# Attention by pairs of units on one core: coarser softmax stages, and a finished tile turned together with its gate logits

## The chip, the core and the metric

The kernel runs on one core of a Trainium2 chip, as one launch. Its time is device time in microseconds (us). TensorE (PE in the profile) multiplies, and its weight loads have a row of their own (PEld). VectorE is DVE, ScalarE is ACT, GpSimd is POOL, and SyncE (SP) issues most DMAs. PE, DVE, ACT and POOL each work through their own instructions in the order in which the kernel writes them.

## The reference, cut to what matters

```
scores = q @ k.T / 8;  bias = -slope[h] * |i - j|;  mask = 0 <= i - j < 128      # B 4, H 8, S 576, D 64
attn   = exp(scores + bias - max);  attn = attn / (sum(attn) + 1e-9);  x = attn @ v   # x: 2304 tokens x 512
logits = x @ w_gate + modality_bias[modality_id];  e = argmax(logits)            # 8 experts
out[e == i] = gate * (relu(x[e == i] @ w1[i]) @ w2[i])
h = out @ w_in;  result = relu(h)**2 @ w_out
```

All of it is float32. The change lies in the first two lines and in `x @ w_gate`.

## The kernel before, in words

The tokens form 18 groups of 128 rows. Each of the four batches has tiles t = 0 to 3 of 128 queries and a tail t = 4 of 64 queries; the tails of two batches share a group. A query sees at most 128 keys back, so a tile t = 1 to 3 needs 256 columns of keys, t = 0 needs 128, and the tail 192 (both heads of a pair lie on the 128 partitions of the tail, 64 queries each).

A **unit** is one tile and one head pair `hp` (two heads of 64 dimensions, which fill 128 partitions), so there are 80 units. The loop over `k` from line 792 is a pipeline written out by hand (the schedule is manual: the order in the code is the order on each engine). In step `k`:

- `sc` of unit k+1 (L220, L223): scores on PE into PSUM. For t < 4 each head is a product over 64 partitions, one on partitions 0 to 63 and one on 64 to 127.
- `smax` of unit k (L234, L236): on DVE scale, bias and row maximum in one instruction for each head, from PSUM into `x`.
- `ev` of unit k-4 (L286 to L289): ACT copies the turned weights of attention from the PSUM bank `x` to `pt`.
- `sexp` of unit k-1 (L249, L252): ACT's exp with its row sum, for each head.
- `tr` of unit k-3 (L275, L277, L278): PE turns the exponentials by 128x128 transposes into the one bank `x`.
- `norm` (L259 to L266): for the tail the division before the product, on DVE; for t < 4 only the 1e-9, on POOL.
- `background()`: one step of each open generator (the `post` of finished tiles, the routing `route`, the prefetch of the first expert).
- `pv` of unit k-5 (L306, L313): PE multiplies by V into one of two banks `v`, 64 columns of weights for each head.

When all four head pairs of a tile are in its bank `v`, `post` takes over: ACT copies the bank to a row buffer `xu` (L330); four transposes (L337) and four products with 16 gate columns (L338, into bank `m`) turn it back to tokens by 512 and give the logits by head; DVE divides both by the row sums (L349, L351), adds the heads up (L352), and SP writes the tokens to DRAM (L354).

All float32 products but the transposes run as two instructions on PE, so a product has two matmul records and two weight loads in the trace. After the loop come five expert slots and a dense layer, whose products all have line 643 in the trace. The first expert's products start inside the last steps of the loop (`FIRST_UP`, `PIECES`); loads of most expert weights start at the loop's end, when the attention's SBUF is given back (L824).

Of the kernel before, what the change touches and what calls it, by code (L numbers as in the profile page):

```python
# [8 lines left out]
F32 = mybir.dt.float32  # L9
# [3 lines left out]
AF = mybir.ActivationFunctionType  # L13
# [35 lines left out]
def attention_moe_kernel(ctx, tc, qh, kh, v, mid, wg, mb, w1, w2, win, wout, out):  # L49
# [9 lines left out]
    def ct(shape, name, dt=F32, p=const):  # L59
        return p.tile(shape, dt, name=name)  # L60
# [40 lines left out]
    wgs = ct([128, 4, 2 * E], "wgs")  # L101
# [16 lines left out]
    wk = ap("wk", 3)  # L118
# [4 lines left out]
    biast = ct([128, 4, 192], "biast", p=cst)  # L123
    mids = ct([128, 2 * NT], "mids", I32, p=cst)
# [87 lines left out]
    def sc(u):  # L212
        b, t, hp = u
        if t < 4:

            st[u] = [bank("s"), bank("t")]
            c0 = 128 if t == 0 else 0
            for j in range(2):
                r = slice(64 * j, 64 * j + 64)
                pe.matmul(st[u][j][:, c0:256], qS[b, t][r, hp, :], kS[b][r, hp, 128 * t - 128 + c0:128 * t + 128], start=True, stop=True)  # L220
        else:
            st[u] = [bank("s")]
            pe.matmul(st[u][0][:, :192], qS[b, t][:, hp, :], kS[b][:, hp, 384:576], start=True, stop=True)  # L223

    def smax(u):
        b, t, hp = u
        s = st[u]
        x = wk.tile([128, 2, 256], F32, tag="x", name="x")
        m = sm.tile([128, 2], F32, tag="m", name="m")
        kw = dict(scale=-0.125, scalar=3e38, op0=ALU.add, op1=ALU.min)  # L230
        if t < 4:
            c0 = 128 if t == 0 else 0
            for j in range(2):
                dve.tensor_tensor_reduce(out=x[:, j, c0:], in0=s[j][:, c0:256], in1=bias[:, 2 * hp + j, c0:], accum_out=m[:, j:j + 1], **kw)  # L234
        else:
            dve.tensor_tensor_reduce(out=x[:, 0, :192], in0=s[0][:, :192], in1=biast[:, hp, :], accum_out=m[:, 0:1], **kw)  # L236
        st[u] = x, m

    def sexp(u):
        b, t, hp = u  # L240
        x, m = st[u]
        st[u] = e = wk.tile([128, 2, 256], F32, tag="e", name="e", bufs=5)
        if t < 4:
            if hp == 0:
                rinv[b, t] = sm.tile([128, H], F32, tag="ri", name="ri")
            c0 = 128 if t == 0 else 0
            for j in range(2):
                h = 2 * hp + j
                act.activation(e[:, j, c0:], x[:, j, c0:], AF.Exp, bias=m[:, j:j + 1], scale=-1.0, accum_out=rinv[b, t][:, h:h + 1])  # L249
        else:  # L250
            rinv[u] = r = sm.tile([128, 1], F32, tag="rt", name="rt")
            act.activation(e[:, 0, :192], x[:, 0, :192], AF.Exp, bias=m[:, 0:1], scale=-1.0, accum_out=r)  # L252

    def norm(u, stage):
        b, t, hp = u
        if t < 4:
            if stage == 0 and hp == 3:
                r = rinv[b, t]
                pool.tensor_scalar(r, r, 1e-9, None, op0=ALU.add)  # L259
        elif stage == 0:  # L260
            dve.tensor_scalar(rinv[u], rinv[u], 1e-9, None, op0=ALU.add)
        elif stage == 1:
            dve.reciprocal(rinv[u], rinv[u])
        else:
            e = st[u]
            dve.tensor_scalar(e[:, 0, :192], e[:, 0, :192], rinv.pop(u), None, op0=ALU.mult)  # L266

    def tr(u):
        b, t, hp = u
        e = st[u]  # L270
        st[u] = p = bank("x", (128, 4, 128))
        if t < 4:
            for j in range(2):
                for i in range(1 if t == 0 else 0, 2):
                    pe.transpose(p[:, 2 * i + j, :], e[:, j, 128 * i:128 * i + 128], ident)  # L275
        else:
            pe.transpose(p[:, 0, :], e[:, 0, 0:128], ident)  # L277
            pe.transpose(p[:64, 1, :], e[:, 0, 128:192], ident)  # L278

    def ev(u):  # L280
        b, t, hp = u
        p = st[u]
        st[u] = o = wk.tile([128, 4, 128], F32, tag="pt", name="pt")
        if t < 4:
            c0 = 2 if t == 0 else 0
            act.copy(o[:, c0:, :], p[:, c0:, :])  # L286
        else:
            act.copy(o[:, 0, :], p[:, 0, :])
            act.copy(o[:64, 1, :], p[:64, 1, :])  # L289
# [4 lines left out]

    def pv(u):
        b, t, hp = u
        o = st.pop(u)
        if hp == 0:
            pvb[b, t] = bank("v", (128, 4, 128))
        w = pvb[b, t]  # L300
        kb = [4] if t == 4 else [t - 1, t] if t else [t]
        if t < 4:
            for n, k_ in enumerate(kb):
                for j in range(2):
                    h = 2 * hp + j
                    pe.matmul(w[64 * j:64 * j + 64, hp, :], vS[b][:, k_, 64 * h:64 * h + 64], o[:, 2 * (k_ - t + 1) + j, :], start=n == 0, stop=n == len(kb) - 1, skip_group_check=True)  # L306
        else:
            c = slice(64 * (b % 2), 64 * (b % 2) + 64)
            for n in range(2):
                r = 64 if n else 128  # L310
                for j in range(2):
                    h = 2 * hp + j
                    pe.matmul(w[64 * j:64 * j + 64, hp, c], vS[b][:r, 3 + n, 64 * h:64 * h + 64], o[:r, n, 64 * j:64 * j + 64], start=n == 0, stop=n == 1, skip_group_check=True)  # L313

        if u[2] == 3:
            if t < 4 or b % 2 == 0:
                xus[group(u)] = row().rearrange("p (a b) -> p a b", a=4)
            if t == 4:
                act.copy(xus[group(u)][:, :, c], w[:, :, c])

    xbusy = []
    xus = {}

    def post(u):
        b, t, _ = u
        g = group(u)
        w = pvb.pop((b, t))
        xu = xus.pop(g)
        if t < 4:
            act.copy(xu, w)  # L330
        yield
        while xbusy:
            yield
        xbusy.append(True)
# [8 lines left out]
        le = "p h e -> p e h"  # L343
        if t == 4:
            dve.tensor_copy(xs, xp.rearrange("p a b -> p (a b)"))
            dve.tensor_reduce(l_all[:, g, :], lp.rearrange(le), axis=AX.X, op=ALU.add)
        else:
            r = rinv.pop((b, t))[:, :, None]
            dve.tensor_tensor(xs.rearrange("p (h d) -> p h d", h=H), xp.rearrange("p a (c d) -> p (a c) d", d=64), r.to_broadcast([128, H, 64]), op=ALU.mult)  # L349
            ls = sm.tile([128, H, E], F32, tag="ls", name="ls", bufs=2)  # L350
            dve.tensor_tensor(ls, lp, r.to_broadcast([128, H, E]), op=ALU.mult)  # L351
            dve.tensor_reduce(l_all[:, g, :], ls.rearrange(le), axis=AX.X, op=ALU.add)  # L352
        xbusy.pop()
# [182 lines left out]
    units = [(b, t, hp) for b in range(B) for t in range(5) for hp in range(4)]  # L536
# [216 lines left out]
    FIRST_UP = 81  # L753
    PIECES = 1
# [37 lines left out]
    for k in range(n + 5):  # L792
        if k + 1 < n:
            sc(units[k + 1])
        if 0 <= k - 2 < n:
            norm(units[k - 2], 0)
        if k < n:
            smax(units[k])
        if 0 <= k - 4 < n:
            ev(units[k - 4])  # L800
        if 0 <= k - 1 < n:
            sexp(units[k - 1])
        if 0 <= k - 3 < n:
            tr(units[k - 3])
        if 0 <= k - 2 < n:
            norm(units[k - 2], 1)
        background()
        if 0 <= k - 2 < n:
            norm(units[k - 2], 2)
        if k % 4 == 1 and k // 4 + 3 < len(tiles):  # L810
            load(*tiles[k // 4 + 3])
        for at, make in ((6, tail_consts), (9, tail_bias), (11, route_consts), (15, logit_bias), (30, dump_rows)):
            if k == at:
                make()
        if 0 <= k - 5 < n:
            u = units[k - 5]
            pv(u)
            if u[2] == 3 and (u[1] < 4 or u[0] % 2):
                todo.append(post(u))
# [335 lines left out]
```

## Time and profile before

| | us |
|---|---|
| median of 3 runs (832.58 to 834.7) | 832.81 |
| the profiled execution | 831.27 |
| its span, first to last instruction | 829.6 |
| PE busy | 801.1 (97%) |
| DVE busy | 397.8 (48%) |
| ACT busy | 342.5 (41%) |
| POOL busy | 274.3 (33%) |

The profiled execution lies 1.54 us below the median. A matmul's record contains the way through the array, so records of neighbours overlap; the distance between two starts tells what one costs. "Busy" counts such an overlap once, and a PE that is busy all the time may still stand between two groups of products.

### The profile page before, as it was taken

How to read it: one execution, taken by the hardware profiler on the slowest of the kernel's cores; microseconds unless marked ns; L12 is line 12 of the kernel's file. 1: busy time of each engine (PE TensorE's matmuls, PEld its weight loads, DVE VectorE, ACT ScalarE, POOL GpSimd, SP SyncE). 2: the span in 40 equal slices, each digit the busy share in tenths (PEclk: the TensorE clock that was granted, in tenths of full speed). 3: DMA queues.
4: the chain of work that ended last, by engine and by line, in shares of the span. 5: the costliest groups of instructions: out<-in, count | busy, mean ns of one | idle time of the engine just before them, and what ended most of it. 6: DMA issues, size and time to landing. Idle time of an engine off the chain costs nothing.

```text
span 829.6 us, 13776 instructions
## 1 busy us (share of the span) xinstructions
PE 801.1 (97%) x5051; PEld 670.5 (81%) x5051; DVE 397.8 (48%) x1060; ACT 342.5 (41%) x910; POOL 274.3 (33%) x330
## 2 busy tenths in 40 slices
PE   6999999999899999989789999999999999999998
PEld 3767676777688788878678989899898989899896
DVE  3676767678988765777345432122221203131220
ACT  5877778534444444444352423223140413222230
POOL 1111033036665556554232432213050413223140
PEclk9999999999999999999899999999999999999999
DMA  6354353138565545462201021010100101010000
GB/s 217 105 176 168 124 177 135 65 115 307 190 237 172 197 167 198 168 207 73 66 22 56 26 77 52 1 52 2 39 14 0 53 0 52 1 51 1 26 1 26
DMA packets 38807, 79.11 MB, mean 95 GB/s; under 512 B 6224, under 2 KB 14672, under 8 KB 38736
## 3 DMA queue, kind: packets, MB, share of 16 engines
q1 hardware_dynamic: 35696, 68.23, 24.7%
q0 software_dynamic: 3040, 9.96, 3.2%
q8 instruction: 41, 0.67, 0.3%
q14 instruction: 30, 0.25, 0.1%
HBM read 62.19 MB, written 15.99 MB: 94 GB/s over the span
## 4 chain that ended last, share of the span: by engine, by line
PE 51%; DVE 0%; ACT 0%; issue 0%; DVEq 0%
PE t L643 19%; PE v L643 15%; PE s L643 13%; PE x L643 2%; PE m L643 1%; PE x L631 1%; PE m L631 0%; DVE w L638 0%; ACT w L636 0%; ACT w L553 0%; ACT row L1015 0%; DVE row L1031 0%; DVE w L989 0%; DVE row L993 0%; DVEq L948 0%
## 5 line engine op out<-in xcount | busy, mean ns | idle before, releaser
L643 PE MATMUL s<-w 128*128 128x256 f32 (+2 forms) x1344 | 220.8, 321 | 7.6 <-DVE h L668 6.9
L643 PEld LDWEIGHTS s<-w 128*128 128x128 f32 x1344 | 194.5, 191 | 27.3 <-DVE h L668 10.0
L643 PE MATMUL t<-w,h 128*128 128x512 f32 x888 | 214.4, 397 | 0.0
L1006 POOL TENSOR_TENSOR h<-row,h 128x256 fp32r<-128x256 f32 x144 | 109.5, 764 | 276.0 <-ACT h L1005 271.3
L643 PEld LDWEIGHTS t<-w,h 128*128 128x128 f32 x888 | 164.4, 188 | 37.8
L643 PE MATMUL v<-w,h 128*128 128x512 f32 x432 | 104.7, 396 | 0.0
L643 PEld LDWEIGHTS v<-w,h 128*128 128x128 f32 x432 | 80.2, 188 | 18.7
L554 POOL TENSOR_TENSOR w<-w 128x1024 fp32r<-128x1024 f32 x23 | 56.8, 2474 | 33.0 <-PE s L643 18.5
L1016 DVE SCALAR_TENSOR_TENSOR row<-s,row 128x256 f32<-128x256 f32 x72 | 30.5, 424 | 70.1 <-ACT row L1015 70.1
L249 ACT ACTIVATE e<-x,m 128x256 f32<-128x256 f32 (+1 forms) x128 | 60.8, 482 | 0.8 <-DVE m L234 0.8
L1005 ACT CAST h<-row 128x256 fp32r<-128x256 f32 x144 | 57.6, 400 | 4.8 <-DVE row L1016 4.8
L638 DVE TENSOR_TENSOR w<-x,w 128x512 fp32r<-128x512 f32 (+1 forms) x13 | 7.7, 606 | 90.6 <-ACT w L636 90.6
L220 PE MATMUL s<-kS,qS 64*128 64x256 f32 (+1 forms) x128 | 44.7, 436 | 6.4 <-DMA qS<-qh 6.1
L553 ACT CAST w<-w 128x1024 fp32r<-128x1024 f32 x46 | 48.0, 1049 | 6.2 <-DVE row L409 2.8
L1015 ACT ACTIVATE row<-s 128x256 f32<-128x256 f32 x72 | 27.5, 383 | 54.7 <-PE s L643 53.6
L643 PE MATMUL t<-w 128*128 128x256 f32 x384 | 48.3, 282 | 0.0
L667 ACT ACTIVATE h<-s 128x512 fp32r<-128x512 f32 (+1 forms) x40 | 23.1, 577 | 61.1 <-PE s L643 58.1
L643 PEld LDWEIGHTS t<-w 128*128 128x128 f32 x384 | 47.1, 190 | 0.3
L636 ACT CAST w<-x 128x512 fp32r<-128x512 f32 (+1 forms) x13 | 6.6, 521 | 96.3 <-PE x L631 96.3
L554 DVE TENSOR_TENSOR w<-w 128x1024 fp32r<-128x1024 f32 x26 | 42.7, 1647 | 6.9 <-ACT w L553 6.3
L286 ACT COPY pt<-x 128x512 f32<-128x512 f32 (+1 forms) x64 | 34.2, 534 | 28.4 <-PE x L275 21.1
L220 PE MATMUL t<-kS,qS 64*128 64x256 f32 (+1 forms) x128 | 44.8, 437 | 0.0
(234 smaller groups left out, 1080.4 us busy)
## 6 DMA issues: line engine op xcount, KB each, us to landing
w<-w SPq DMA_DIRECT2D x40, 512.0 KB
w<-win SPq DMA_DIRECT2D x16, 512.0 KB
w<-wout SPq DMA_DIRECT2D x16, 512.0 KB
xd<-row SPq DMA_DIRECT2D x22, 256.0 KB
qS<-qh SPq DMA_DIRECT2D x19, 256.0 KB
row<-yd SPq DMA_DIRECT2D x18, 256.0 KB
vS<-vh SPq DMA_DIRECT2D x16, 256.0 KB
out_dram<-row SPq DMA_DIRECT2D x16, 256.0 KB
```

What stands on the lines that cost most here:

```text
L220: pe.matmul(st[u][j][:, c0:256], qS[b, t][r, hp, :], kS[b][r, hp, 128 * t - 128 + c0:128 * t + 128], start=True, stop=True)
L249: act.activation(e[:, j, c0:], x[:, j, c0:], AF.Exp, bias=m[:, j:j + 1], scale=-1.0, accum_out=rinv[b, t][:, h:h + 1])
L286: act.copy(o[:, c0:, :], p[:, c0:, :])
L553: (dve.tensor_copy if quick else act.copy)(h, r)
L554: (eng or dve).tensor_tensor(l, r, h.bitcast(F32), op=ALU.subtract)
L631: pe.transpose(p[:, c, :], r[:, 128 * c:128 * c + 128], ident)
L643: pe.matmul(ps, l, r, start=first and i == 0, stop=last and i == n - 1)
L667: act.activation(hh, p, AF.Relu)
L1005: act.copy(g[:, 0:256], gt)
L1006: pool.tensor_tensor(g[:, 256:512], gt, g[:, 0:256].bitcast(F32), op=ALU.subtract)
L1015: act.activation(r, p, AF.Relu)
L1016: dve.scalar_tensor_tensor(gt, p, 0.0, r, op0=ALU.max, op1=ALU.mult)
```

## The change

The unit becomes a pair of head pairs, (b, t, hh): 40 units instead of 80. Scores of two head pairs lie in one bank (`s` and `t` are now full banks), transposes go to two banks `v`, one for each head pair, and the product with V goes to one bank `W0` that is kept for good. The pipeline has three stages fewer: `smax` and `sexp` belong to the same step, `tr` and `ev` come two steps later, `pv` three. `post` copies the tile with DVE instead of ACT, and turns it and makes its logits in one product for each head pair: the moving operand is the identity and 16 gate columns side by side, 144 columns. Three of these land in bank `m`, the fourth in the upper half of `W0`; DVE then needs two divisions from each of the two banks.

```
-    for k in range(n + 5):
-        sc(k+1); norm(k-2, 0); smax(k); ev(k-4); sexp(k-1); tr(k-3); norm(k-2, 1); background(); norm(k-2, 2); pv(k-5)
+    for k in range(n + 3):
+        smax(units[k])
+        sexp(units[k], 0)
+        norm(units[k - 1])
+        sc(units[k + 1])
+        tr(units[k - 2])
+        ev(units[k - 2], 0)
+        sexp(units[k], 1)
+        ev(units[k - 2], 1)
+        background()
+        pv(units[k - 3])
+        background()
```

The block above leaves out the bounds on k and the loads; the lines below are the diff's.

```
-    wk = ap("wk", 3)
+    wk = ap("wk", 2)
+    turned = ct([128, 4, 128 + 2 * E], "turned", p=cst)
...
-        nc.sync.dma_start(out=wgs, in_=wg)
+        nc.sync.dma_start(out=turned[:, :, 128:], in_=wg)
+        for i in range(4):
+            pool.tensor_copy(turned[:, i, :128], ident)
...
+    W0 = bank("x", (128, 4, 128))
...
-        if t < 4:
-            act.copy(xu, w)
+        dve.tensor_copy(xu[:, :, c], W0[:, :, c])
+        if t == 4 and b % 2 == 0:
+            return
...
-        xp, lp = w, bank("m", (128, H, E))
+        C = 128 + 2 * E
+        xp = bank("m")[:, :3 * C].rearrange("p (a c) -> p a c", a=3), W0[:, 2:4, :].rearrange("p a b -> p (a b)")[:, None, :C]
         for i in range(4):
-            pe.transpose(xp[:, i, :], xu[:, i, :], ident)
-            pe.matmul(lp[:, 2 * i:2 * i + 2, :], xu[:, i, :], wgs[:, i, :], start=True, stop=True)
+            pe.matmul(xp[i // 3][:, i % 3, :], xu[:, i, :], turned[:, i, :], start=True, stop=True)
...
+        for p, h0, n in ((xp[0], 0, 6), (xp[1], 6, 2)):
+            hs = slice(h0, h0 + n)
+            for o, w, d in ((xs.rearrange("p (h d) -> p h d", h=H)[:, hs, :], p[:, :, :128], D), (ls[:, hs, :], p[:, :, 128:], E)):
...
+                    dve.tensor_tensor(o, w, r[:, hs].rearrange("p (a j) -> p a j", j=2)[:, :, :, None].to_broadcast([128, n // 2, 2, d]), op=ALU.mult)
...
-    FIRST_UP = 81
-    PIECES = 1
+    FIRST_UP = 40
+    PIECES = 2
```

The next two pieces are PE's order where the scores of the second batch's tail begin: first the last steps of t = 3 with the turn of tile t = 1 before the change (`s`, `t` scores, `e` exponentials, `pt` turned, `m` logits; numbers tell buffers apart).

```order
L220 MATMUL s_1083<-kS_359,qS_730 128x256
L220 MATMUL t_1084<-kS_359,qS_730 128x256
L275 MATMUL x_1096<-ident_71,e_1040 128x128 x4
L337 MATMUL v_956<-ident_71,row_1052 128x128
L338 MATMUL m_1101<-wgs_89,row_1052 128x16
...
L306 MATMUL v_1078<-pt_1062,vS_360 64x128 x4
L223 MATMUL s_1115<-kS_359,qS_851 128x192
L275 MATMUL x_1126<-ident_71,e_1064 128x128 x4
L306 MATMUL v_1078<-pt_1091,vS_360 64x128 x4
```

The same place after the change, one step with the turn of tile t = 1 (`x_123` is `W0`).

```order
L226 MATMUL s_971<-kS_335,qS_765 128x192 x2
L289 MATMUL v_974<-ident_71,e_861 128x128 x4
L289 MATMUL v_979<-ident_71,e_861 128x128 x4
L353 MATMUL m_989<-turned_117,row_956 128x144 x3
L353 MATMUL x_123<-turned_117,row_956 128x144
L324 MATMUL x_123<-pt_943,vS_336 64x128 x8
```

Scores, turns and products with V now stand in groups of two head pairs, so PE goes from one kind to the next half as often; the eight instructions of the turn have become four.

ACT at the same place before: the copy of the tile, evictions, and exps of the unit whose maxima were found a step earlier.

```order
L330 COPY row_1052<-v_956 128x512
L286 COPY pt_1091<-x_1068 128x512
L249 ACTIVATE e_1093,ri_1065<-x_1058,m_1059 128x256 x2
L286 COPY pt_1121<-x_1096 128x512
L249 ACTIVATE e_1123,ri_1065<-x_1087,m_1088 128x256 x2
```

ACT after the change:

```order
L260 ACTIVATE e_922,ri_923<-x_916,m_917 128x256 x2
L300 COPY pt_943<-v_933 128x512
L260 ACTIVATE e_922,ri_923<-x_916,m_917 128x256 x2
L300 COPY pt_943<-v_938 128x512
L260 ACTIVATE e_968,ri_923<-x_962,m_963 128x256 x2
```

The exps now stand ahead of the step's evictions and need maxima of the same step; the copy of the tile is gone from this queue. It stands on DVE, ahead of the next step's maxima, and the turn's results are taken by four divisions instead of two:

```order
L344 COPY row_956<-x_123 128x512
L239 ISA x_962,m_963<-s_927,bias_115 128x256
...
L355 RECIPROCAL ri_728<-ri_728 128x8
L367 TENSOR_TENSOR row_1003<-m_989,ri_728 128x384
L367 TENSOR_TENSOR ls_1004<-m_989,ri_728 128x48
L367 TENSOR_TENSOR row_1003<-x_123,ri_728 128x128
L367 TENSOR_TENSOR ls_1004<-x_123,ri_728 128x16
L368 TENSOR_REDUCE l_all_72<-ls_1004 128x8
```

Before, DVE had at this place only the divisions and the sum:

```order
L340 RECIPROCAL ri_841<-ri_841 128x8
L234 ISA x_1117,m_1118<-s_1083,bias_116 128x256
...
L349 TENSOR_TENSOR row_1131<-v_956,ri_841 128x512
L351 TENSOR_TENSOR ls_1133<-m_1101,ri_841 128x64
L352 TENSOR_REDUCE l_all_72<-ls_1133 128x8
```

## Rows read from the trace of the kernel before

**Rows 1.** Windows: us busy by engine, instructions, granted clock, DMA share, GB/s.
```profile
core 0: us, PE busy (x) PEld busy (x) DVE busy (x) ACT busy (x) POOL busy (x), PEclk, DMA share, GB/s
22.00:160.00 138.00, 136.36 (x1257) 98.66 (x1253) 95.90 (x491) 106.67 (x372) 23.05 (x54) 1.00 0.42 139
160.00:240.00 80.00, 76.16 (x369) 60.07 (x368) 66.31 (x149) 32.81 (x54) 41.38 (x31) 1.00 0.58 206
```

**Rows 2.** Timeline, PE: start, duration, line, tiles, shape. One step, scores of t = 3.
```profile
66.81 0.48 PE L220 MATMUL s<-kS,qS 64*128 64x256 f32 x1
67.13 0.38 PE L220 MATMUL s<-kS,qS 64*128 64x256 f32 x1
67.45 0.66 PE L275 MATMUL x<-ident,e 128*128 128x128 f32 x4
68.03 0.66 PE L306 MATMUL v<-pt,vS 128*64 128x128 f32 x8
68.62 0.48 PE L220 MATMUL s<-kS,qS 64*128 64x256 f32 x1
```

**Rows 3.** Timeline, PE: scores of 128 columns, t = 0.
```profile
78.81 0.37 PE L220 MATMUL s<-kS,qS 64*128 64x128 f32 x1
79.02 0.27 PE L220 MATMUL s<-kS,qS 64*128 64x128 f32 x1
79.23 0.33 PE L277 MATMUL x<-ident,e 128*128 128x128 f32 x1
```

**Rows 4.** Timeline, PE: first units of the kernel, four units' scores in one run.
```profile
3.77 0.55 PE L220 MATMUL s<-kS,qS 64*128 64x128 f32 x1 [3.77 <-DMA qS<-qh]
4.11 0.42 PE L220 MATMUL s<-kS,qS 64*128 64x128 f32 x1
4.33 0.42 PE L220 MATMUL s<-kS,qS 64*128 64x128 f32 x1
4.54 0.42 PE L220 MATMUL s<-kS,qS 64*128 64x128 f32 x1
```

**Rows 5.** Timeline, PE: units of a tail, t = 4.
```profile
71.53 0.59 PE L223 MATMUL s<-kS,qS 128*128 128x192 f32 x2
71.95 0.60 PE L275 MATMUL x<-ident,e 128*128 128x128 f32 x4
72.48 0.66 PE L306 MATMUL v<-pt,vS 128*64 128x128 f32 x8
```

**Rows 6.** Timeline, PE: the turn of a finished tile.
```profile
69.25 0.66 PE L275 MATMUL x<-ident,e 128*128 128x128 f32 x4
69.75 0.27 PE L337 MATMUL v<-ident,row 128*128 128x128 f32 x1
69.86 0.29 PE L338 MATMUL m<-wgs,row 128*128 128x16 f32 x2
70.00 0.31 PE L337 MATMUL v<-ident,row 128*128 128x128 f32 x1
70.94 0.66 PE L306 MATMUL v<-pt,vS 128*64 128x128 f32 x8
```

**Rows 7.** Timeline, ACT: an eviction and a unit's two exps.
```profile
70.00 0.58 ACT L286 COPY pt<-x 128x512 f32<-128x512 f32 x1
70.48 0.51 ACT L249 ACTIVATE e<-x,m 128x256 f32<-128x256 f32 x1
70.99 0.50 ACT L249 ACTIVATE e<-x,m 128x256 f32<-128x256 f32 x1
```

**Rows 8.** Timeline, DVE: a unit's two maxima, with the wait ahead of them.
```profile
67.66 0.42 DVE L234 CUSTOM_DVE_ANT_0 x<-s,bias 128x256 f32<-128x256 f32 x1 [1.03 <-PE t L220]
68.01 0.42 DVE L234 CUSTOM_DVE_ANT_0 x<-t,bias 128x256 f32<-128x256 f32 x1
```

**Rows 9.** Groups by line and form, DVE, 18 to 160 us: busy, mean ns, idle before.
```profile
L349 DVE TENSOR_TENSOR row<-v,ri 128x512 f32<-128x512 f32 x15 | 10.4, 692 | 11.0 <-PE v L337 4.3 <-ACT pt L286 4.2 <-PE t L220 1.7
L352 DVE TENSOR_REDUCE l_all<-ls 128x8 f32<-128x64 f32 x15 | 4.0, 267 | 0.5
L351 DVE TENSOR_TENSOR ls<-m,ri 128x64 f32<-128x64 f32 x15 | 3.2, 215 | 0.0
L345 DVE COPY row<-v 128x512 f32<-128x512 f32 x1 | 0.7, 691 | 0.5 <-PE v L337 0.5
```

**Rows 10.** Waits, 22 to 160 us: total us, times, longest.
```profile
DVE x L234 <- PE t L220: 15.5, 27, 1.0
PEld x L275 <- ACT pt L286: 8.9, 21, 1.0
```

More of the change, by code (lines that the diff above doesn't have):

```diff
@@ L254, in norm @@
[L254 to L257, printed above, removed]
+                h = 4 * hh + 2 * i + j
+                act.activation(e[:, i, j, c0:], x[:, i, j, c0:], AF.Exp, bias=m[:, i, j:j + 1], scale=-1.0, accum_out=rinv[b, t][:, h:h + 1])
+        else:
+            act.activation(e[:, i, 0, :192], x[:, i, 0, :192], AF.Exp, bias=m[:, i, 0:1], scale=-1.0, accum_out=rinv[u][:, i:i + 1])
+        if i:
+            st[u] = ex.pop(u)
+    def norm(u):
+        b, t, hh = u
+        if t < 4:
+            if hh:
@@ L268, in tr @@
+        dve.reciprocal(r, r)
+        for i in range(2):
+            dve.tensor_scalar(e[:, i, 0, :192], e[:, i, 0, :192], r[:, i:i + 1], None, op0=ALU.mult)
     def tr(u):
-        b, t, hp = u
+        b, t, hh = u
         e = st[u]
[L271 to L283, printed above, removed]
+        st[u] = ps = []
+        for i in range(2):
+            p = bank("v", (128, 4, 128))
+            ps.append(p)
+            if t < 4:
+                for j in range(2):
+                    for k_ in range(1 if t == 0 else 0, 2):
+                        pe.transpose(p[:, 2 * k_ + j, :], e[:, i, j, 128 * k_:128 * k_ + 128], ident)
+            else:
+                pe.transpose(p[:, 0, :], e[:, i, 0, 0:128], ident)
+                pe.transpose(p[:64, 1, :], e[:, i, 0, 128:192], ident)
@@ L284, in ev @@
+        ex[u] = wk.tile([128, 2, 4, 128], F32, tag="pt", name="pt")
+    def ev(u, i):
+        b, t, hh = u
+        p, o = st[u][i], ex[u]
         if t < 4:
             c0 = 2 if t == 0 else 0
[L286 removed]
+            act.copy(o[:, i, c0:, :], p[:, c0:, :])
         else:
[L288 to L289 removed]
+            act.copy(o[:, i, 0, :], p[:, 0, :])
+            act.copy(o[:64, i, 1, :], p[:64, 1, :])
+        if i:
+            st[u] = ex.pop(u)
@@ L534, in attention_moe_kernel @@
     second = []
-    units = [(b, t, hp) for b in range(B) for t in range(5) for hp in range(4)]
+    units = [(b, t, hh) for b in range(B) for t in range(5) for hh in range(2)]
     tiles = [(b, t) for b in range(B) for t in range(5)]
@@ L791, in attention_moe_kernel @@
     hidden = []
-    for k in range(n + 5):
+    for k in range(n + 3):
+        now, last = k < n, 0 <= k - 2 < n
+        if now:
+            smax(units[k])
+            sexp(units[k], 0)
+        if 0 <= k - 1 < n:
+            norm(units[k - 1])
         if k + 1 < n:
             sc(units[k + 1])
[L795 to L806, printed above, removed]
-        background()
[L808 to L812, printed above, removed]
+        if last:
+            tr(units[k - 2])
+            ev(units[k - 2], 0)
+        if now:
+            sexp(units[k], 1)
+        if last:
+            ev(units[k - 2], 1)
+        background()
+        if k >= 3:
+            pv(units[k - 3])
+        background()
+        if k % 2 == 0 and k // 2 + 3 < len(tiles):
+            load(*tiles[k // 2 + 3])
+        for at, make in ((3, tail_consts), (4, tail_bias), (5, route_consts), (7, logit_bias), (15, dump_rows)):
             if k == at:
                 make()
[L815 to L819, printed above, removed]
         if k >= FIRST_UP and primed:
```

141 lines of the change are left out of this document (66 added, 75 removed).

## The prediction

> **What bounds the kernel now.** I read the windows first. From 22 to 160 us, the attention, PE is busy for 136.4 of 138 us, DVE for 95.9 and ACT for 106.7 [rows 1]. So PE decides here, and what it is busy with has to be read from the distances between starts. The timeline of one step shows them: scores start at 66.81, turns at 67.45, products with V at 68.03, the next scores at 68.62 [rows 2]: 0.64 + 0.58 + 0.59 = 1.81 us for each unit. None of the three is filled. The turn's eight instructions follow each other in 0.11 us (69.75, 69.86) [rows 6], and the four transposes of the tail's step span 0.60 us with a last one of about 0.27 [rows 5, 6], again 0.11 apart, so four need 0.44 us and get 0.58. The eight of V span 0.66 us [rows 2], with the same last one 0.056 apart; they need 0.45 and get 0.59. Scores of 256 columns take 0.32 for each of the two instructions of a head (66.81, 67.13, 67.45) [rows 2] and of 128 columns 0.21 (78.81, 79.02, 79.23) [rows 3]: 0.11 us for 128 columns and 0.10 on top of every instruction. What is too long always comes where PE goes over to products of another shape: 64 rows for the scores, 128x128 for the turns, 128x64 for V. In the tail, where scores and turns have one shape, two scores of 192 columns take 0.42 [rows 5], which is 2 x 0.16 by columns and 0.10 left for one change. Of the waits, PE's own one for data is small: 8.9 us for the bank `x` in 21 places [rows 10], a part of which is the same change of shape.
>
> **The change, part by part.**
>
> *Fewer changes of shape.* A unit of t < 4 has three, together 0.14 (before V) + 0.14 (after V) + 0.21 (around the scores) = 0.49 us; a tail unit has two. Counted in the order of instructions up to the first expert, it is 223 changes before and 119 after; among the latter are 11 new ones, where routing or the first expert's turns now follow V. So 104 go, at 0.49 / 3 = 0.163 us: 17.0 us. The disputed part is the 0.21 around the scores. If the 0.10 on top belongs to each instruction, a pair of head pairs pays it as before, and only 0.28 of 0.49 is saved: 104 x 0.093 = 9.7 us. The startup speaks against that: four units' scores stand there in one run, the first instruction takes 0.34 (3.77 to 4.11), the next ones 0.22 and 0.21 [rows 4], so only the first carries the extra. These rows are of the slow start of the kernel, where 0.21 us is twice what 128 columns cost later, so the proof is not complete; I take 17.0 and keep 9.7. The Trainium skill, "TensorEngine Tiling (Array Packing)", Key Properties, says that changing the tiling mode drains TensorE, and a change of tile within a mode does not; by that rule all of the extra is the change's and this term is the 17.0, by the other reading of the warm rows 9.7.
>
> *The start.* Up to 22 us the PE rows are slower and the first loads are waited for (3.77 us) [rows 4]. I count nothing for the first four pairs: 4 x 0.5 = 2 us back.
>
> *The turn with the logits.* Before, from 69.75 to 70.94, 1.19 us with the change to V in it; without the 0.14 it is 1.05, about 0.09 for each of twelve instructions. After, four products of 144 columns, each of two instructions. By the slope of rows 2 and 3 one takes 144 x 0.105 / 128 = 0.12, eight 0.95: 0.1 us won for each of 18 groups, 1.8 us. Upper bound: 0.105 each as for a transpose of 128 columns, 0.84, 3.8 us won. Lower bound: 0.21 as the tail's scores with their change counted in [rows 5], 1.68, 11.3 us lost. I take 1.8, since rows 6 show loads of 128x128 weights every 0.09 us and so no reason for 0.21.
>
> *What goes to DVE.* The copy of the tile (0.69 us as in the one copy of this size [rows 9]) moves from ACT to DVE: 16 full and 4 half ones, 12.5 us. The two divisions become four; the columns are the same, so what is added is two fixed shares: 0.15 us each, from 0.215 for 64 columns against 0.692 for 512 [rows 9], so 18 x 0.3 = 5.4 us. DVE goes from 95.9 to 113.8 us in a stretch which, after the terms above, has about 120 us. It was 69% busy (95.9 of 138) and is then 95%. That is near enough to full that its order matters. By steps of a tile of t = 1 to 3, from the end of its V products: copy 0.25 to 0.9; maxima of the next pair (four, 0.35 us apart [rows 8]) to 2.3; then the divisions, which wait for the turn's products on PE (scores 1.05, transposes 1.0, turn 0.95, so 3.2) and take 1.35 us to 4.6; next maxima to 6.0; and PE reaches the end of the tile's second step at about 7.1. ACT needs 0.48 for an eviction and 0.51 for an exp [rows 7], four exps and two evictions for a pair, 3.0 us; its exps start at 5.4, when the first maxima are there, and its last eviction ends at 8.4, and PE wants it at 8.7, behind the next scores and transposes. So it just fits, with 0.3 us in hand, and routing (some 20 small DVE instructions for three tiles) falls mostly into DVE's two idle pieces (2.3 to 3.2 and 6.0 to 7.3). What does not fall there PE waits for. From both sides: nothing, or 20 tiles x 0.55 = 11 us, if all the idle time that DVE has in front of the divisions (11.0 us in 15 places [rows 9]) has to be kept. I take 4, by the 0.3 us in hand.
>
> *The rest.* The four POOL copies for the moving operand and the loads on SP stand in the first steps, where POOL is nearly idle (23 of 138 us later [rows 1]): nothing, at most 1 us. The bank `x` that PE waited for is now two banks `v`: 0 to 4 us won, and I take 0, since the turn of the first expert now needs the same two banks. What follows the attention keeps its order and starts with it; PE is the busiest there too (76.2 of 80 us, DVE 66.3 [rows 1]), and the loads of the expert weights start when the loop ends, so I let it shift as a whole.
>
> Sum: -17.0 + 2 - 1.8 + 4 = -12.8 us. The profiled execution of 831.27 becomes 818.5; it stands 1.54 below the median of 832.81, so on the median's scale **820 us**.
>
> **The rivals.**
>
> *DVE and ACT become the bound.* For it: 95% of DVE, exps that now need maxima of the same step, evictions behind the exps, one bank `W0` that must be copied before the next V products. Against it: DVE waits for PE's scores now (15.5 us in 27 places [rows 10]) and that time can be filled. Worked out: DVE's 113.8 us, and 20 us that stay idle because every tile waits once 1 us for its turn's products, make 134 of the 138 us: a gain of 4 to 7 us, 826 to 829. The Trainium skill, "TensorEngine Tiling (Array Packing)", PSUM Bottleneck, warns of this: after a faster TensorE the copies out of PSUM may bound, and both ACT and DVE should take them; here DVE takes the tile's copy alone, and no run here shows yet what that does.
>
> *The extra belongs to instructions, not to changes.* Then 9.7 instead of 17.0: 827. For it: 0.32 twice in a row in rows 2. Against it: rows 4 and the tail.
>
> *Slower: PE waits in each tile for the copy of `W0`.* One bank holds the result of V; PE can't go on with the next tile's V until DVE has read it, and the copy stands in DVE's queue behind routing and the divisions, which wait for PE themselves. In my steps the copy ends at 0.9 us and V wants the bank at 3.2 + 0.2, so 2.5 us are in hand. It decides from the point where DVE runs 2.5 us late. At 3.5 us late (one tile's copy, divisions and maxima, 0.65 + 1.35 + 1.4, not caught up) PE stands 1.0 us in each of 20 tiles, 20 us: 820 + 20 = 840.
>
> *No change.* The turn at its lower bound (11.3 lost instead of 1.8 won) takes the gain nearly away: 820 + 13.1 = 833.
>
> **How the numbers follow.** The forecast 0.55 (813 to 825), DVE and ACT 0.18, the extra by instruction 0.10, the turn 0.06, the wait for `W0` 0.11. About 0.3% of the time, 2.5 us, is what can be told from no change. The first three are faster by more than that, the 829 of the second just so: 0.82 for faster, 0.07 for the same (the turn, and a little of the second), 0.11 for slower. The range runs from 809 (no wait of PE instead of 4 us, no loss at the start instead of 2, the turn at 3.8 won: 820 - 8 = 812, and 3 of the up to 4 us of the second bank) to 830, which takes in the second and third case; the wait for `W0` and part of the turn stay outside.
>
> **What would show it.** In the profile after: scores of two head pairs at 0.21 us an instruction inside a group and 0.10 to 0.2 more at its ends; eight transposes in 1.0 us, sixteen V instructions in 1.0; eight instructions of the turn in 0.95. Steps of a pair of about 3.1 us, 4.1 with a turn. The stretch that ends at 160 us here ends near 147. PE waits for ACT's evictions below 5 us in all. Wrong it would be if PE shows waits for `pt` or for `row` copied from `W0` in every tile, if DVE stands between 95 and 100% while PE's groups have holes, or if the gain at the end of the attention shrinks before 400 us.

## The result, and the profile after

The changed kernel takes 825.16 us (median; 823.71 to 828.75) against 832.69 us for the kernel before on the same chip: a ratio of 0.9916, 95% interval 0.9892 to 0.9940. Run twice more beside the experiments it gave 0.9932 (0.9908 to 0.9957) and 0.9908 (0.9883 to 0.9934). So it is faster by 0.8%, about 7.5 us, inside the range and short of the 820 us by 5. The 12.8 us of the forecast came to little more than half, and the question is where the rest went.

The windows of the changed kernel answer to [rows 1]; columns as there.

```profile
core 0: us, PE busy (x) PEld busy (x) DVE busy (x) ACT busy (x) POOL busy (x), PEclk, DMA share, GB/s
22.00:160.00 138.00, 130.29 (x1231) 103.76 (x1230) 108.84 (x546) 95.45 (x348) 20.23 (x42) 0.99 0.42 142
160.00:240.00 80.00, 72.80 (x317) 57.49 (x316) 67.92 (x131) 31.63 (x51) 46.43 (x33) 0.98 0.60 211
```

PE is no longer full: 7.7 us idle of 138, and 7 of 80 behind. The groups themselves came as worked out. PE's timeline of the changed kernel, a turn, a tail step and scores of 256 columns, answers to [rows 2, 5, 6] (of the scores the instructions of one bank):

```profile
61.70 0.90 PE L353 MATMUL m<-turned,row 128*128 128x144 f32 x6
62.44 0.41 PE L353 MATMUL x<-turned,row 128*128 128x144 f32 x2
62.77 1.09 PE L324 MATMUL x<-pt,vS 128*64 128x128 f32 x16
...
64.55 1.04 PE L289 MATMUL v<-ident,e 128*128 128x128 f32 x8
65.52 1.09 PE L324 MATMUL x<-pt,vS 128*64 128x128 f32 x16
66.54 0.37 PE L224 MATMUL s<-kS,qS 64*128 64x128 f32 x1
...
72.80 0.48 PE L224 MATMUL s<-kS,qS 64*128 64x256 f32 x1
73.12 0.38 PE L224 MATMUL s<-kS,qS 64*128 64x256 f32 x1
73.33 0.38 PE L224 MATMUL s<-kS,qS 64*128 64x256 f32 x1
73.55 0.38 PE L224 MATMUL s<-kS,qS 64*128 64x256 f32 x1
73.86 0.33 PE L291 MATMUL v<-ident,e 128*128 128x128 f32 x1
```

Inside a group a score instruction takes 0.21 us (73.12 to 73.33), at the ends 0.32 and 0.31; eight transposes take 0.97 (64.55 to 65.52), sixteen V instructions 1.02, the turn's eight 1.07 (61.70 to 62.77, foretold 0.95).

To see where time is won and lost, the span is cut at five events that every kernel has, each read from the timeline: the start of DVE's small reduction of `l_all` for the first finished tile and for the tenth, the start of the first up product of the first expert (PE, `s<-w`), the start of its first down product (PE, `t<-w,h`), and the end. All are profiled runs, us. Each row is one execution, and a kernel's median can lie apart from it: e_third's profiled run is 3.8 us above its median, so small differences between rows carry no weight alone.

| kernel | to tile 1 | tiles 1 to 10 | to first up | up to down | rest | span |
|---|---|---|---|---|---|---|
| before | 27.1 | 74.0 | 59.1 | 28.8 | 640.6 | 829.6 |
| changed | 25.1 | 66.6 | 58.3 | 34.2 | 641.0 | 825.1 |
| changed, e_again | 24.4 | 66.6 | 59.1 | 34.2 | 641.0 | 825.3 |
| changed, e_third | 24.4 | 66.6 | 56.9 | 34.4 | 642.5 | 824.7 |
| e_split | 25.0 | 73.8 | 62.0 | 29.9 | 643.2 | 833.9 |
| e_turn | 23.8 | 67.5 | 59.7 | 30.0 | 642.8 | 823.8 |
| e_cast | 23.7 | 66.6 | 58.9 | 35.8 | 642.4 | 827.4 |
| e_bankt | 24.5 | 66.6 | 59.9 | 29.8 | 641.3 | 822.0 |
| e_late | 24.5 | 66.6 | 59.2 | 30.9 | 646.4 | 827.5 |
| e_dve | 23.2 | 66.6 | 56.2 | 31.5 | 639.2 | 816.7 |
| e_copy | 24.0 | 66.8 | 53.6 | 29.7 | 643.1 | 817.1 |
| e_both | 24.0 | 66.8 | 55.0 | 31.2 | 637.9 | 814.8 |
| e_warm | 22.7 | 66.6 | 56.8 | 29.8 | 643.3 | 819.2 |
| b_dve | 27.5 | 74.0 | 58.4 | 29.4 | 637.6 | 826.8 |

The changed kernel wins 2.0 us at the start and 7.4 over nine tiles, then only 0.8 in the second half of the attention, where the first expert is prepared, and it gives back 5.4 between the first up and the first down product. In the second half the loss stands in one interval, from the thirteenth finished tile to the fourteenth, in which the first expert's rows are turned: 16.7 us before, 19.9 in the changed kernel and 20.2 in e_third, whose other intervals up to the sixteenth tile are all shorter than before. The sum, -4.4, is that of the two profiled spans (829.6 to 825.1); the medians lie 7.5 apart, since the profiled run of before was 1.4 us below its median and that of the changed kernel (826.8) 1.6 above.

The place of the 5.4 is seen in PE's waits of the changed kernel from 160 to 200 us (total, times, longest), in DVE's and POOL's timelines and in PE's:

```profile
PE m L435 <- DVE row L431: 3.5, 2, 2.6
PE x L646 <- DMA row<-xd,idx: 0.4, 1, 0.4
```

```profile
171.13 1.35 DVE L426 SCALAR_TENSOR_TENSOR row<-row 128x1 f32<-128x1 f32 x1
172.71 2.36 DVE L431 TENSOR_SCALAR row<-iota,row 128x128 fp32r<-128x128 f32 x1
```

```profile
170.08 2.39 POOL L569 TENSOR_TENSOR w<-w 128x1024 fp32r<-128x1024 f32 x1 [6.48 <-ACT w L568]
172.66 2.34 POOL L569 TENSOR_TENSOR w<-w 128x1024 fp32r<-128x1024 f32 x1 [0.19 <-ACT w L568]
```

```profile
171.27 1.21 PE L658 MATMUL s<-w 128*128 128x512 f32 x4 [0.27 <-DVE h L683]
175.13 0.50 PE L435 MATMUL m<-row 128*128 128x160 f32 x1 [2.65 <-DVE row L431]
175.43 3.29 PE L658 MATMUL s<-w 128*128 128x512 f32 x8
```

Both DVE instructions end with POOL's split of a weight chunk: 172.48 beside 172.47, 175.07 beside 175.00. PE stands 2.65 us for the second, and the eight products behind it take 3.29 us: the granted clock is 1.00 from 172 to 174 us and 0.50, the lower level of 1.2 GHz, from 175 to 178, where 0.58 is the mean from 174 to 178. PE's other wait for that row, 0.86 us at 163.7, has the same look: a TENSOR_SCALAR of 128x128 runs from 161.27 to 163.68 beside a split from 161.12 to 163.60. The two waits and the 1.2 us that the eight products take beyond e_late's 2.06 make 4.7 of the 5.4 us.

### The profile page after: what moved, and what is told of

Its sections match the earlier page's. It is cut to its first block, busy times and chain, and to the rows that moved or that the text cites. A ratio compares the mean times of both kernels' runs of the same rounds, so it can differ in the third digit from the quotient of the medians.

```text
span 825.1 us, 13566 instructions
## 1 busy us (share of the span) xinstructions
PE 785.6 (95%) x4979; PEld 671.3 (81%) x4979; DVE 410.4 (50%) x1102; ACT 331.3 (40%) x890; POOL 275.5 (33%) x334
## 4 chain that ended last, share of the span: by engine, by line
PE 51%; DMA 0%; ACT 0%; DVE 0%; issue 0%; SPq 0%; DVEq 0%
PE t L658 19%; PE v L658 15%; PE s L658 12%; PE x L658 2%; PE m L658 1%; PE m L646 1%; PE x L646 0%; DMA row<-yd 0%; DVE w L653 0%; ACT w L651 0%; ACT w L568 0%; DVE row L1043 0%; DVE w L569 0%; ACT row L1027 0%; SPq L992 0%
## 5 line engine op out<-in xcount | busy, mean ns | idle before, releaser
L260 ACT ACTIVATE e<-x,m 128x256 f32<-128x256 f32 (+1 forms) x128 | 60.6, 476 | 29.8 <-DVE m L239 29.4
L569 POOL TENSOR_TENSOR w<-w 128x1024 fp32r<-128x1024 f32 x23 | 56.9, 2475 | 40.9 <-PE s L658 19.9
L682 ACT ACTIVATE h<-s 128x512 fp32r<-128x512 f32 (+1 forms) x40 | 23.1, 577 | 67.5 <-PE s L658 60.0
L651 ACT CAST w<-x 128x512 fp32r<-128x512 f32 (+1 forms) x13 | 6.6, 522 | 98.4 <-PE x L646 98.4
L604 POOL TENSOR_TENSOR w<-w,row 128x512 int32<-128x512 int32 x18 | 26.1, 1451 | 51.4 <-DVE row L603 39.2
L224 PE MATMUL s<-kS,qS 64*128 64x256 f32 (+1 forms) x128 | 36.0, 408 | 7.2 <-DMA qS<-qh 7.2
L683 DVE SCALAR_TENSOR_TENSOR h<-s,h 128x512 fp32r<-128x512 f32 (+1 forms) x40 | 26.2, 658 | 24.2 <-ACT h L682 20.2
```

The lines of the kernel that those rows point to most:

```text
L224: pe.matmul(s[j][:, i, c0:], qS[b, t][r, hp, :], kS[b][r, hp, 128 * t - 128 + c0:128 * t + 128], start=True, stop=True)
L260: act.activation(e[:, i, j, c0:], x[:, i, j, c0:], AF.Exp, bias=m[:, i, j:j + 1], scale=-1.0, accum_out=rinv[b, t][:, h:h + 1])
L569: (eng or dve).tensor_tensor(l, r, h.bitcast(F32), op=ALU.subtract)
L604: pool.tensor_tensor(a, a, r, op=ALU.add)
L682: act.activation(hh, p, AF.Relu)
L683: dve.scalar_tensor_tensor(hl, p, 0.0, hh.bitcast(F32), op0=ALU.max, op1=ALU.subtract)
```

## The experiments

Ratios are to the kernel before in the same batch. The changed kernel was e_again in the first batch and e_third in the third; the second batch had none, so its kernels are held against the three ratios above, 0.992 on average.

**e_again and e_third: the changed kernel itself.**

> The changed kernel once more, unaltered, beside the next three on the same chip, as the mark for effects below 1%. All theories: 823 to 828 us, ratio to the kernel before 0.989 to 0.994, and the wait of PE for the row maxima near 175 us (2.65 us) there again.

> The changed kernel once more, unaltered, as the mark beside the next three on the same chip. All theories: ratio to the kernel before 0.990 to 0.994.

Measured: 826.19 us, 0.9932, and 822.82 us, 0.9908, as expected. The wait near 175 us is in both, at 2.57 and 2.5 us.

**e_split: the groups cut in two again.**

```diff
-            sc(units[k + 1])
+            sc(units[k + 1], (0,))
...
-            tr(units[k - 2])
+            tr(units[k - 2], (0,))
...
+            pv(units[k - 3], (0,))
+            sc(units[k + 1], (1,))
+            tr(units[k - 2], (1,))
...
-            pv(units[k - 3])
+            pv(units[k - 3], (1,))
```

> The joined groups are cut in two again: four score products, four transposes, eight V products of one head pair, then the same of the other, so that PE changes shape six times a step in place of three, with the same instructions, the joined turn kept and the same delay of two stages. Theory 1 (the gain is the fewer changes of shape, about 0.16 us each, some 100 in the attention): each step gets 0.4 to 0.5 us longer where PE is busy throughout, the lead over the kernel before at the end of attention falls from 10 to 0 to 2 us, the time is 833 to 842 us, no gain left. Rival (the extra time belongs to the instructions, not to the changes): within 3 us of the changed kernel (823 to 828).

Measured: 835.59 us, 1.0072 (1.0042 to 1.0101), slower than before. Nine tiles take 73.8 us, as before the change, in place of 66.6: 0.80 us a tile, 0.40 a step, 0.13 for each of three changes. The groups by line and form from 22 to 100 us show it for V, in e_split, the changed kernel and before (busy us, mean ns):

```profile
L331 PE MATMUL x<-pt,vS 128*64 128x128 f32 x240 | 20.6, 287 | 0.0
```

```profile
L324 PE MATMUL x<-pt,vS 128*64 128x128 f32 x272 | 19.0, 280 | 0.0
```

```profile
L306 PE MATMUL v<-pt,vS 128*64 128x128 f32 x236 | 20.4, 287 | 0.0
```

In groups of eight an instruction costs 0.086 us (20.6 / 240, 20.4 / 236), in groups of sixteen 0.070. The instructions are the same as in the changed kernel, and PE waits for no other engine longer than 0.2 us from 27 to 98 us, so waits that the new order might bring are not the reason: the extra belongs to the changes. The Trainium skill, "TensorEngine Tiling (Array Packing)", Key Properties, says that changing the tiling mode drains TensorE. The trace agrees that a change costs, 0.13 us here; the drain itself no row shows.

**e_turn: the joined product of 144 columns taken apart.**

```diff
-            pe.matmul(xp[i // 3][:, i % 3, :], xu[:, i, :], turned[:, i, :], start=True, stop=True)
+            pe.transpose(xp[i // 3][:, i % 3, :128], xu[:, i, :], ident)
+            pe.matmul(xp[i // 3][:, i % 3, 128:], xu[:, i, :], turned[:, i, 128:], start=True, stop=True)
```

> Four products of 144 columns per finished tile become four transposes of 128 columns and four products of 16 columns, into the same banks, all else as in the changed kernel. Theory 1 (the turn costs what its instructions take, 1.07 us for the eight and about 1.05 for twelve at 0.09, and the gain is by the grouping of steps): within 1.5 us of the changed kernel. Rival (the joined product is where the gain came from): 4 to 8 us slower. Second rival (the joined product is a loss that eats up the gain): 2 to 5 us faster.

Measured: 823.47 us, 0.9917 (0.9887 to 0.9947). Nine tiles take 0.9 us more, 0.1 a tile: what the joined product is worth. Yet the run is not slower than e_again, because its up-to-down stretch is 30.0 us in place of 34.2: a microsecond later, only the small instruction of DVE's row met POOL's split (1.35 us). That was the first hint that the loss there is a matter of phase.

**e_late: one split put off.**

```diff
-                advance_split(min(4 + f // 2, 6 if "left" in wpools else 4))
+                advance_split(min(4 + f // 2, 5 if "left" in wpools else 4))
```

> The last split of a weight chunk that the first up product starts ahead (one more chunk in flight) is put off to the down product. Theory 1 (part of the gain is lost between 162 and 178 us because VectorE's TENSOR_SCALAR of the splits stands beside POOL's, so that the row maxima come 2.65 us late and PE's clock falls to 0.58 behind it): that wait goes, the granted clock there is 1.00, the time is 3 to 4 us below the changed kernel (821 to 822 us). Rival (the chunk has to be split at some place, and the wait goes with it): the wait stands again later, the time is within 1 us of the changed kernel. Second rival (the missing part is lost elsewhere, by products that were never as many or as dear as counted): within 1 us, although the wait is gone.

Measured: 827.58 us, 0.9958 (0.9940 to 0.9976), not faster than e_again. The wait of 2.65 us went (0.64 left) and up to down fell by 3.3 us, with the clock at 1.00 from 174 to 178 us. But the rest grew by 5.4 us. DVE, POOL and PE of e_late:

```profile
182.99 2.38 DVE L527 SCALAR_TENSOR_TENSOR r<-r,r,siota 1x11 f32<-1x11 f32 x1
```

```profile
182.93 2.42 POOL L569 TENSOR_TENSOR w<-w 128x1024 fp32r<-128x1024 f32 x1 [10.13 <-ACT w L568]
```

```profile
192.43 0.66 PE L646 MATMUL x<-ident,row 128*128 128x128 f32 x4 [2.74 <-DMA row<-xd,idx]
```

The split moved, and the next routing instruction to meet it, one row of 11 elements that takes 0.21 us alone, stood 2.38 us. That row of instructions ends in the gather for the second expert, which PE now reached first and waited 2.74 us for. My theory that the wait at 175 us was the loss was too narrow; the rival, that the wait stands again later, was right, though the median came 1.4 us above e_again's and not within 1. What delays PE there is DVE's routing row, wherever the split meets it. Another 2.6 us of e_late's lead go near 400 us (see the end of the next section).

**e_cast: weight casts of the first expert on ACT.**

```diff
-            wsplit(key, None, pool if (j % 2 if s else j > 0) else None, chunk_sides(s, j), s == 0 and j < 3)
+            wsplit(key, None, pool if (j % 2 if s else j > 0) else None, chunk_sides(s, j), False)
```

> The casts of the first expert's first three weight chunks go from VectorE to ScalarE. Theory 1 (the other loss, some 4 us between 114 and 134 us, is VectorE being late with the row maxima while it also casts and splits weights): the lead over the kernel before at 134 us grows by 1 to 3 us, the time falls by 1 to 3 us. Rival (ScalarE with its exps is the late one there): the lead shrinks, 1 to 4 us slower. Second rival (the loss there comes from the turns of the prefetched expert waiting for banks): no change, within 0.7 us.

Measured: 825.37 us, 0.9936 (0.9912 to 0.9960), no change; the stretch to the first up product is 58.9 us beside e_again's 59.1. Moving three casts of 0.69 us from DVE to ACT brings nothing. It met the split a third way (DVE, POOL):

```profile
171.92 2.31 DVE L427 TENSOR_TENSOR row<-row,idc 128x1 f32<-128x1 f32 x1
```

```profile
169.48 4.74 POOL L569 TENSOR_TENSOR w<-w 128x1024 fp32r<-128x1024 f32 x2 [6.65 <-DMA w<-w]
```

**e_dve: the splits of chunks 4 to 7 on DVE; b_dve: the same in the kernel before.**

```diff
-            wsplit(key, None, pool if (j % 2 if s else j > 0) else None, chunk_sides(s, j), s == 0 and j < 3)
+            wsplit(key, None, pool if (j % 2 if s else 0 < j < 4) else None, chunk_sides(s, j), s == 0 and j < 3)
```

> The splits of the first expert's second four weight chunks go from POOL to VectorE (1.22 us each there, 2.4 us on POOL). Theory 1, as the previous runs leave it (any VectorE instruction that meets POOL's split of 128x1024 stands until that ends; this holds up the row of small routing instructions that ends in the gather for the second expert, and so PE): VectorE's TENSOR_SCALAR of 128x128 takes 0.35 us there again in place of 2.36 and the 128x1 one 0.15 in place of 1.35, no wait of PE over 1.3 us between 160 and 193 us, the time is 1.5 to 3 us below the changed kernel. Rival (those instructions are slow for another reason, such as the transfers running beside them): they keep their 2.3 us, the time is 0 to 3 us above.

> The kernel before, with the splits of the first expert's chunks 4 to 7 on VectorE instead of POOL and nothing else changed. Theory 1 (the meeting of VectorE's routing row with POOL's splits is in the kernel before too, but costs less there, since its 128x1 instruction took 1.35 us and its three 128x128 ones 1.85 us, and the gather came 190.3 to 195.1 us): 0 to 2.5 us faster than the kernel before. Rival (the edit is worth 3 to 4 us in any kernel, so that what it gives the changed kernel says nothing of the change): 3 us or more faster.

Measured: e_dve 819.37 us, 0.9882 (0.9855 to 0.9908), about 3 us below the changed kernel by the ratios; b_dve 829.85 us, 0.9981 (0.9962 to 0.9999), 1.2 us below before. Groups of e_dve, DVE from 160 to 192 us, and PE's waits from 160 to 200:

```profile
L431 DVE TENSOR_SCALAR row<-iota,row 128x128 fp32r<-128x128 f32 x1 | 0.3, 347 | 0.0
...
L426 DVE SCALAR_TENSOR_TENSOR row<-row 128x1 f32<-128x1 f32 x1 | 0.1, 148 | 0.0
```

```profile
PE s L658 <- DVE h L683: 1.6, 2, 1.2
PE m L435 <- DVE row L431: 0.8, 1, 0.8
PE x L646 <- DMA row<-xd,idx: 0.5, 1, 0.5
```

With POOL's splits gone, the two instructions take 0.35 and 0.15 us in place of 2.36 and 1.35, and no wait passes 1.2 us. POOL's split was the cause. In the kernel before the same edit leaves up to down as it was (28.8 and 29.4 us): the meeting cost little there. It is the change that brought it onto PE's path. Not all of e_dve's gain is of this kind: behind the first down product the edit wins time in both kernels (the column "rest", 640.6 to 637.6 and 641.0 to 639.2), and only the 2.7 us between up and down are the changed kernel's own.

**e_bankt: another bank for the prefetched expert's turns.**

```diff
-            turn(0, i, xr[0][1][i], "v")
+            turn(0, i, xr[0][1][i], "t")
```

> The four turns of the prefetched expert take the second score bank instead of the banks that the softmax transposes now use. Theory 1 (of the 4 us lost between 114 and 134 us, the waits of 1.14 and 1.22 us for the eviction of the softmax transposes are a part that the sharing of these banks makes): those two waits go, the lead at 145 us grows by 1 to 2.5 us, and of that 0 to 2 us arrive at the end. Rival (VectorE and ScalarE are late there whatever the bank): the wait turns up at the scores or at the turn, the lead at 145 us stays within 0.7 us.

Measured: 825.29 us, 0.9954 (0.9933 to 0.9974), not faster. The two waits for the eviction went and others came, in e_bankt from 100 to 136 us:

```profile
PE t L224 <- DVE w L653: 2.4, 3, 1.2
PE t L646 <- issue: 1.8, 1, 1.8
```

To the first up product it took 59.9 us against e_third's 56.9. The rival is right in kind: the engines that empty the banks are late there, whichever bank it is. The lead at that point was 3 us smaller than e_third's, though, where the rival had it unchanged.

**e_copy: the tile's copy back on ACT.**

```diff
-        dve.tensor_copy(xu[:, :, c], W0[:, :, c])
+        act.copy(xu[:, :, c], W0[:, :, c])
```

> The copy of a finished tile's 128x512 result goes from VectorE to ScalarE. Theory 1 (PE bounds the attention, with VectorE and ScalarE mostly behind cover): within 2 us of the changed kernel. Rival (VectorE, which grew from 95.9 to 108.8 us busy of 138, bounds the attention now): 3 to 8 us faster. Second rival (ScalarE sets the tile's turn): 2 to 6 us slower.

Measured: 818.02 us, 0.9855 (0.9829 to 0.9881), about 5 us below the changed kernel: more than my theory allowed, and in the rival's range. But the rival placed it in the attention, and there nothing moved: nine tiles take 66.8 us, 0.2 more. The gain is in the stretch to the first up product, 53.6 us against 56.9 in e_third, and in up to down, 29.7, where the split met only one small instruction (1.36 us). Windows 92 to 150 us of e_third, then of e_copy:

```profile
92.00:150.00 58.00, 52.63 (x492) 42.26 (x491) 46.09 (x222) 38.61 (x140) 12.34 (x18) 0.97 0.40 135
```

```profile
92.00:150.00 58.00, 54.36 (x518) 43.60 (x517) 44.53 (x227) 42.37 (x151) 12.29 (x18) 1.00 0.41 139
```

DVE is busy for 46.1 of 58 us and yet late. The waits of ACT and DVE from 92 to 150 us in e_third, then ACT's in e_copy, show why:

```profile
ACT e L260 <- DVE m L239: 11.2, 8, 2.4
DVE w L653 <- ACT w L651: 4.5, 2, 2.6
```

```profile
ACT e L260 <- DVE m L239: 7.4, 5, 2.1
```

ACT's exps wait for DVE's maxima. DVE stands 4.5 us for ACT's copy of the first expert's turned rows (L651), with the next maxima behind it in its queue, while that copy stands in ACT's queue behind exps that wait for the maxima before. Two queues hold each other up there; in the kernel before, DVE's longest wait for that copy is 0.9 us. Taking 0.69 us a tile off DVE shortens ACT's wait, not this one (4.5 us in e_copy too), and keeps PE busier by 1.7 us and its clock at 1.00 in place of 0.97. No run moves the two instructions, so what that wait costs is not shown.

**e_both: e_dve and e_copy together.** (Both diffs above.)

> The changed kernel with two edits of earlier runs together: the splits of the first expert's chunks 4 to 7 on VectorE, and the copy of a finished tile on ScalarE. Theory 1 (both take the same thing away, VectorE's lateness while POOL splits and the routing runs, so that their gains overlap): ratio 0.984 to 0.988, 3 to 7 us below the changed kernel, no better than 2 us below the better of the two. Rival (they act at different places and add up): ratio below 0.982.

Measured: 816.44 us, 0.9824 (0.9799 to 0.9849), the fastest of all, 6.4 us below e_third in the same batch. The ratio lies between what the two theories gave and its interval reaches into both, so whether the gains overlap stays open; the profiled spans, 816.7 and 817.1 alone and 814.8 together, lie nearer to an overlap. Of the table, 55.0 us to the first up product is e_copy's part, 637.9 in the rest e_dve's.

**e_warm: PE kept busy before the second tile's scores.**

```diff
+    w = bank("v", (128, 4, 128))
+    for i in range(12):
+        pe.transpose(w[:, i % 4, :], ident, ident)
```

> Twelve transposes of the identity, whose result nothing reads, stand in PE's row behind the first unit's scores, where PE waits 2.9 us for the second tile's q; all else as in the changed kernel. Theory 1 (PE's products run slowly at the start, 0.63 us a 64x256 product until 13.35 us and 0.38 us from 14.35 us, because PE had idled, and the changed kernel got to the fast ones 7 us sooner than the one before because its first groups leave no gap): the 64x256 products take 0.38 us from at least 2 us earlier, and the time is 1 to 2.5 us below the changed kernel. Rival (the speed-up comes at a given time or by something else than PE's work): the fast products start at 14 us again, and the time is within 0.7 us of the changed kernel or up to 0.5 us above.

Measured: 820.88 us, 0.9880 (0.9854 to 0.9905), 1.9 us below e_third beside it, whose interval overlaps. PE's timeline of e_third, then of e_warm (one bank):

```profile
5.36 0.42 PE L224 MATMUL s<-kS,qS 64*128 64x128 f32 x1
...
9.65 0.63 PE L224 MATMUL s<-kS,qS 64*128 64x256 f32 x1
...
12.21 0.63 PE L224 MATMUL s<-kS,qS 64*128 64x256 f32 x1
...
13.84 0.38 PE L224 MATMUL s<-kS,qS 64*128 64x256 f32 x1
```

```profile
4.78 2.82 PE L784 MATMUL v<-ident 128*128 128x128 f32 x12
...
7.87 0.27 PE L224 MATMUL s<-kS,qS 64*128 64x128 f32 x1
...
9.02 0.38 PE L224 MATMUL s<-kS,qS 64*128 64x256 f32 x1
```

The same product takes 0.38 us from 9 us on in place of 0.63 until 12.2. The first tile is done 1.7 us earlier. PE's work before, not the clock on the wall, brings the fast products. The whole 1.9 us of the median can't be put down to this, since the run also met the split at a harmless moment (29.8 us up to down, against 34.4).

## Why the prediction was right, and where not

- *Fewer changes of shape, -17.0.* Right in kind, a little too large: e_split puts the price at 0.13 us a change (0.163 foretold), 0.80 us a tile, 14.4 for 18 tiles if all ran like the first ten. The rival by which the extra belongs to each instruction fell.
- *The turn, -1.8.* e_turn measures 0.1 us a tile, 1.8 for 18. The rival that it costs the gain fell.
- *The start, +2.* Wrong in sign: -2.0 to -2.7. I charged it by the slow rows [rows 4] and did not ask why they were slow. In the changed kernel the fast products come at 14.4 us; before, a product took 0.63 us until 21 us. e_warm shows that PE's earlier work brings them forward. Which feature of the changed kernel's work does it is not shown: from 9.2 us to the fast products PE's rows have no idle time in the kernel before and none in e_third, only longer groups after the change.
- *DVE and ACT waits, +4.* Near in size, wrong in place. I spread it over all tiles. In tiles 1 to 10 little is lost (PE waits for DVE twice, 1.6 us), and the steps I timed by hand held; PE's waits for ACT's evictions are 2.7 us from 22 to 160 us in its own row, and 5.8 in that of the weight loads, in which [rows 10] counted 8.9, a little above the 5 foretold. Nearly all of it falls in the second half: that stretch holds six turned tiles and 39 fewer changes of shape, where the first nine tiles had nine and 48, so at their rate it would win an estimated 5 to 6 us; it won 0.8 to 2.2 (the changed kernel's profile and e_third), 3 to 5 less. e_copy gets 3.3 of it back. So the rival "DVE and ACT become the bound" is right for the half in which the first expert's work stands in the same queues, though by their order: DVE is at 79%, not the 95% foretold. I had put routing into DVE's idle pieces and counted nothing for the expert's turned rows. The Trainium skill, "TensorEngine Tiling (Array Packing)", PSUM Bottleneck, advises that both engines take the copies out of PSUM. Both do in either form of the changed kernel; e_copy's 0.6% shows that it matters which takes the tile's copy.
- *"What follows the attention keeps its order and starts with it [...], so I let it shift as a whole."* This is the step that failed: 5.4 us are lost between up and down product. DVE's routing row and POOL's splits stand there in the order of before; before, they met where PE did not wait; shifted, they met on its path (b_dve against e_dve). The prediction named the sign (a gain at the end of the attention that shrinks before 400 us): the lead was 10.3 us at the first up product (13 foretold) and 4.9 at the first down product.
- *The wait for `W0`* did not come: PE waits for a copied tile once, 0.5 us, and that for its turn.

The forecast came out right to 5 us because the gains and the waits were nearly of the right size and the errors partly cancelled, which is luck: the start 4 us better, the changes of shape 3 us worse and the stretch behind the first up product 5.4 us worse. By the number alone the result does not choose between the theories: 825.16 lies 0.2 us outside the forecast's own 813 to 825 and 0.8 below the 826 to 829 of "DVE and ACT become the bound". It is e_split that makes the main term safe.

Two things stay open. Near 112 us DVE waits once for a product of PE, 2.4 to 3.1 us in five profiled runs (the changed kernel's, e_again, e_late, e_turn, e_cast) and at most 0.6 us in the other runs of the changed kernel's order, e_third among them, which is the same program; PE's records show no reason. The five are the changed kernel's own and all of the first batch, and no run of the other two batches has it, so it goes with the batch and not with the edits. And 1.7 to 2.8 us of lead are lost around 400 us in most kernels (e_copy, e_late and e_third among them) and 0.2 to 0.5 in others (the changed kernel's, e_again). PE's clock is a part of it: from 370 to 420 us its granted mean is 0.86 in those three and 0.90 in the changed kernel's and before. Why it differs between runs of one program is not shown.

## What to carry to other kernels

Group TensorE's products by shape: here a change costs 0.13 us, and the three fewer in each step are worth 0.40. Before letting what follows a faster stage "shift as a whole", look for two long rows on DVE and POOL that run beside each other there, since a shift decides where they meet, and take the split off POOL where a chain of small DVE instructions ends in something PE waits for. When a kernel's copies move to an engine, check its worst stretch, not its mean: DVE at 79% was late only where other work, and waits for ACT, stood ahead in its queue.

## What the runs showed of the hardware

- Some DVE instructions on SBUF that meet POOL's 128x1024 TENSOR_TENSOR stand until that ends, whatever their size: 128x128 (2.36 us, alone 0.35), 128x1 (2.31, alone 0.16), 1x11 (2.38, alone 0.21), each ending within 0.1 us of POOL's. Not all do: in the changed kernel a RECIPROCAL of 128x8 in SBUF at 133.08 us took its usual 0.20 inside a split (131.33 to 133.70 us), and DVE's instruction that reads the product from PSUM (L683, 170.53 us) its usual 0.69. The Trainium skill, "SBUF — State Buffer", section "SBUF: two separate sides", says that the two engines share a pair of ports as an exclusive lock for the length of an instruction, which a DVE instruction needs when it has two inputs in SBUF or runs in a 2-port mode. The trace agrees: the 128x1 and the 1x11, with two inputs in SBUF, were held, the RECIPROCAL and L683 not. Which mode the 128x128 TENSOR_SCALAR runs in no row shows. I should have weighed that rule in the prediction.
- At the kernel's start the granted clock is shown as 1.00 (2.4 GHz), while a 64x256 product takes 0.63 us in place of 0.38. The column does not show the slow start: the trace holds no record of the clock before 14.2 us (21.2 in the kernel before, 7.8 in e_warm), about where the fast products begin. The durations show it, and twelve transposes whose result nothing reads end it early in e_warm.
- In a wait of PE of 2.65 us the granted clock fell, and it was at 0.50 (1.2 GHz) for the next 3 us; eight products took 3.29 us instead of 2.06 (e_late, where that wait was 0.64 us). That wait cost more than its length.
